# A fused windowed-attention and feed-forward kernel on one core: one pair of weight blocks less is decoded ahead of the feed-forward, its list opens with eight of its own steps, and two small additions move from GpSimd to VectorE

## The chip, the core and the metric

One core of one Trainium2 chip runs the whole kernel. The metric is the device time of one launch in microseconds, the median over the runs shown. The engines are TensorE (PE, with its weight loads as PEld), VectorE (DVE), ScalarE (ACT), GpSimd (POOL) and SyncE (SP, which only issues DMAs here).

## The reference

Attention over 4 batches, 8 heads, 768 positions, head size 64, with a window of 128 keys and 4 sink keys. Its output goes, as 3072 rows of 512, through a feed-forward of width 2048 with a piecewise activation:

```python
scores = scale * np.matmul(q, k.transpose(0, 1, 3, 2))
scores = np.where(is_sink | in_window, scores, -1000000000.0)
a = np.exp(scores - np.max(scores, axis=-1, keepdims=True))
a = a / (np.sum(a, axis=-1, keepdims=True) + 1e-09)
x = np.matmul(a, v)                      # -> rows of 512
h = x @ w_in
g = np.where(h >= 1, h, np.where(h <= -1, 0.0, (h + 1) ** 2 / 4))
out = g @ w_out
```

The two weight matrices arrive as 64-bit floating-point numbers.

## The kernel before, in words

**Units and chunks.** A unit is a batch, a head and a half of the queries (three tiles of 128). Eight units, all heads of one batch and half, make a chunk, and there are eight chunks. The attention of chunk c+1 runs beside the feed-forward of chunk c. Units 0 to 15 (chunks 0 and 1) are worked as eight pairs with plain fp32 matmuls (`pair_scores`, `early_transp`, `pair_r`, `pair_av`); from unit `NATIVE` = 16 on each unit is worked alone with operands split in a high and a low part (`load`, `scores`, `transp`, `av`).

**Weights.** The 64-bit weights are decoded on the chip, two blocks at a time, in 16 steps: step n is a pair of blocks of `w_in` for even n and of `w_out` for odd n. A step (`weights`, `decode_parts`, lines 158 to 218) is three integer operations on VectorE (shift L164, sign L170, tail L173), a cast on ScalarE (high part, L174) and a subtraction on VectorE (rest, L177). Its `fetch` also issues the DMA of the raw words of later steps. Steps 0 to `WFIRST`-1 are taken apart and woven by hand into `first_pairs`, where `queue` fixes the order on VectorE and ScalarE; a later step is one call, whose shift is held behind whatever VectorE work was written before it (L166).

**The opening.** `first_pairs` (L504) runs pairs 0 to 3 whole and the scores of pair 4. In round m it transposes pair m-1's probabilities, computes pair m's scores, and does half a decode step and the second half of the previous one.

**The lists.** From then on the order on TensorE is the order of the program. Two lists of (weight, step) are merged by `spread` (L615): the feed-forward's steps, and the attention's steps placed between them in proportion to their weights. For chunk 0 the feed-forward's list is `moe_steps` (four `split`s of weight 0, then for each of 16 blocks j four `stage1` steps of weight 0.49, and from j = 2 on three `stage2` steps of block j-2 of weight 0.65), and the remaining decode steps, of weight 1.0 each, are spread into it first (L657, lead 0.9). In the merged list of chunk 0 the first attention entries stand ahead of the first decode step; the first matmuls are the transposes of pair 4's first unit, then `stage1` of block 0. `stage1` of blocks 2p and 2p+1 needs decode step 2p.

**The other engines.** On VectorE, ScalarE and GpSimd a list scheduler picks the order at build time; on the chip each engine runs its instructions in that order and waits at the first that isn't ready. In PSUM, `stage1` has two banks (`h_ps`), which `pair_scores(4, ..)` uses too for two of its six score tiles.

**Around unit 16.** `scores(u, i)` (L266) ends, for the third tile, with the row sums: 1e-9 is added to the three sums on GpSimd (L289), VectorE takes reciprocals (L290) and scales the probabilities (L296, L298, L301), and `transp(u)` (L336) transposes them on TensorE. GpSimd also has the subtraction for the high and low parts of q (L263), of k for units 16 to 19 (L261, `KL_POOL`), and, for chunk 0, of the activation (L577, `GL_POOL`).

Of the kernel before, what the change touches and what calls it, by code (L numbers as in the profile page):

```python
# [13 lines left out]
ALU = mybir.AluOpType  # L14

B, H, S, D = 4, 8, 768, 64
# [3 lines left out]
CT = 3  # L20
NSINK = 4
KB = P + NSINK
NCT = DM // P
# [5 lines left out]
NATIVE = 16  # L29
# [3 lines left out]


CHECK = range(24, 24 + 2 * NJ)
WFIRST = 4
AHEAD = 2
SYNC = 4

# [1 line left out]
LEAD = 0.9  # L41
# [8 lines left out]
def attn_ffn(ctx, tc, qk, qkp, vx, vs, par, w_in, w_out, out):  # L50
    nc = tc.nc
# [12 lines left out]
    def queue(i, on=True):  # L64
        if on:
            e = i.ins.engine
            if e in queued:
                tc.add_manual_dep(i.ins, queued[e].name, mybir.DependencyInfo(
                    mybir.DependencyClass.NoSync, mybir.DependencyReason.DATA), reason="queue")
            queued[e] = i.ins  # L70
        return i
# [116 lines left out]
    def weights(n):  # L188
# [12 lines left out]
        def parts(on):  # L201
            j, i = n // 2 * 2, n % 2
            words = raw[n].rearrange("p j (c two) -> p j c two", two=2)
            if i:
                t = wpool.tile([P, 2, 2, DM], F32R, name="w")
                w_o[j:j + 2] = t[:, 0], t[:, 1]
            else:
                t = wi2[n // 2]
            return decode_parts(t, dec.tile([P, 2, DM], I32, name=f"bits{n % 2}"), words, pin=not on, on=on)
# [5 lines left out]

        if n < WFIRST:
            return fetch, lambda: parts(True)
# [48 lines left out]
    def scores(u, i):  # L266
        b, h, t0 = u
        qs, k_s = st["qk", u]
        if i == 0:
            st["p", u] = [att.tile([P, CT, 260], F32, name="p"), att.tile([P, 2 * CT], F32, name="stat")]  # L270
        p, stat = st["p", u]
        t = t0 + i
        lo = KB if t == 0 else 0
        c0 = i * KB if t0 else max(0, (i - 1) * KB)
        ps = ps_a.tile([P, 512], F32, name="ps_a")
        for j, q in enumerate(qs):
            nc.tensor.matmul(ps[:, lo:260], lhsT=q[:, i * P:(i + 1) * P], rhs=k_s[:, c0:c0 + 260 - lo],  # L277
                             start=(j == 0), stop=(j == len(qs) - 1))
        peak_i = peak[:, units.index(u), i:i + 1]
        m = (m0, m1, m2)[min(t, 2)]  # L280
        nc.vector.tensor_tensor_reduce(  # L281
            out=p[:, i, lo:260], in0=ps[:, lo:260], in1=m, scale=-0.125, scalar=3.0e38,
            op0=ALU.add, op1=ALU.min, accum_out=peak_i)
        nc.scalar.activation(p[:, i, lo:260], p[:, i, lo:260], AF.Exp, bias=peak_i, scale=-1.0,  # L284
                             accum_out=stat[:, i:i + 1])
        if i < CT - 1:
            return
        st.pop(("qk", u))
        nc.gpsimd.tensor_scalar(stat[:, CT:2 * CT], stat[:, 0:CT], 1.0e-9, None, op0=ALU.add)  # L289
        nc.vector.reciprocal(stat[:, CT:2 * CT], stat[:, CT:2 * CT])  # L290
        i0 = int(t0 == 0)

        for i in range(CT):
            r, own = stat[:, CT + i:CT + i + 1], p[:, i, KB:260]
            if t0 + i == 0:
                nc.vector.tensor_scalar(own, own, r, None, op0=ALU.mult)  # L296
            else:
                nc.vector.tensor_tensor_reduce(out=own, in0=own, in1=p[:, i, 0:P], scale=r, scalar=0.0,  # L298
                                               op0=ALU.add, op1=ALU.add, accum_out=stat[:, i:i + 1])
        sk = att.tile([P, CT * NSINK], F32, name="sk")[:, :(CT - i0) * NSINK]  # L300
        nc.vector.tensor_tensor(sk.rearrange("p (i s) -> p i s", s=NSINK), p[:, i0:, P:KB],  # L301
                                stat[:, CT + i0:2 * CT].unsqueeze(2).broadcast_to([P, CT - i0, NSINK]), op=ALU.mult)
        st["p", u] = (p, sk)
# [96 lines left out]
    def pair_values(m):  # L400
        v_s = vq[m % 2]
        for a in range(2):
            b, h, _ = units[2 * m + a]
            nc.sync.dma_start(v_s[:, :CT, a], vx[b, h, :, :CT])
            nc.sync.dma_start(v_s[:NSINK, CT, a], vs[b, h, :NSINK])

    def early_p(u):

        return (p0[u % 2] if u // 2 % 2 == 0 else pt0[u % 2][:, 5 * P:5 * P + CT * 260]).rearrange(
            "p (i c) -> p i c", c=260)  # L410
# [38 lines left out]
    def early_transp(u, part):  # L449

        p, pt = early_p(u), pt0[u % 2]
        on = u < H
        ps = ps_a.tile([P, 512], F32, name="ps_a")
        for n, (i, c) in enumerate((((0, KB), (1, 0), (1, KB)), ((2, 0), (2, KB)))[part]):
            nc.tensor.transpose(ps[:, n * P:(n + 1) * P], p[:, i, c:c + P], ident)
        if part:
            nc.tensor.transpose(ps[:NSINK, 2 * P:CT * P], p[:, CT - 1, P:KB], ident)
            queue(nc.scalar.copy(pt[:, CT * P:5 * P], ps[:, :2 * P]), on)
            queue(nc.scalar.copy(spn[u % 2][:NSINK], ps[:NSINK, 2 * P:CT * P]), on)
        else:  # L460
            queue(nc.scalar.copy(pt[:, :CT * P], ps[:, :CT * P]), on)

    def pair_av(m):

        T = CT * P
        v_s = vq[m % 2]
        ps = ps_a.tile([P, 512], F32, name="ps_a")

        terms = [(2, 4, 1, 2), (0, 0, 2, 0), (1, 2, 2, 1), None]
        for n, t in enumerate(terms):  # L470
            for a in range(2):
                k, s0, ns, i = t or (CT, 0, 1, CT - 1)
                rhs = pt0[a][:, s0 * P:(s0 + ns) * P] if t else spn[a]
                nc.tensor.matmul(ps[a * D:a * D + D, i * P:(i + ns) * P], lhsT=v_s[:, k, a], rhs=rhs,  # L474
                                 start=(n == 0), stop=(n == len(terms) - 1))
        x = xn[:, units[2 * m][1] // 2, :]
        return lambda: queue(nc.vector.tensor_tensor(x, ps[:, :T], x, op=ALU.mult), m < H // 2)
# [26 lines left out]
    def first_pairs():  # L504
        pair_load(0)
        pair_load(1)
        pair_values(0)
        d = None
        for m in range(H // 2 + 1):
            if m:  # L510
                pair_load(m + 1)
                pair_values(m)
                for u in (2 * m - 2, 2 * m - 1):
                    for part in range(2):
                        early_transp(u, part)
            if m == H // 2:
                pair_r(m - 1)
                d[2]()
                pair_av(m - 1)()
            pair_scores(m, 0)  # L520
            pair_scores(m, 1)
            if 0 < m < H // 2:
                d[2]()
            pair_scores(m, 2)
            if m:
                d[3]()
            if 0 < m < H // 2:
                pair_r(m - 1)
            pair_sums(m)
            if m < H // 2:  # L530
                wsteps[m][0]()
                d = wsteps[m][1]()
                d[0]()
                if m:
                    pair_av(m - 1)()
                d[1]()


    chunks = [(b, t) for t in (0, CT) for b in range(B)]
    last = chunks[-1][0] * S + chunks[-1][1] * P  # L540
    units = [(b, h, t0) for b, t0 in chunks for h in range(H)]
# [73 lines left out]
    def spread(a, b, lead=1.0):  # L615

        wa, wb = (sum(w for w, _ in s) for s in (a, b))
        steps, n, da, db = [], 0, 0.0, 0.0
        for step in b:
            while n < len(a) and da * lead * wb <= db * wa:  # L620
                steps.append(a[n])
                da += a[n][0]
                n += 1
            steps.append(step)
            db += step[0]
        return steps + a[n:]
# [14 lines left out]
    for c in range(len(chunks)):  # L641
        n1 = min(H * (c + 1), len(units)) + 2
        if c == 1:
            attn = [step for m in range(5, 9) for step in pair_steps(m)]
            attn += [step for n in range(NATIVE, n1) for step in attn_steps(n)]
        elif c > 1:
            attn = [step for n in range(n0, n1) for step in attn_steps(n)]
        n0 = n1
        for _, f in spread(attn, prev, LEAD) if c else [(0.0, first_pairs)]:
            f()  # L650
        if c == 1:
            early.close()
            chk.append(fast.enter_context(tc.tile_pool(name="chk", bufs=2)))
        b, t0 = chunks[c]
        prev = moe_steps(b * S + t0 * P, tail)
        if c == 0:
            prev = spread([(1.0, f) for f in wsteps[WFIRST:]], prev, WLEAD)  # L657

# [70 lines left out]
    with tc.If(other_v > 0):  # L729
        with tc.tile_pool(name="gen", bufs=1) as gen:  # L730

            for n in range(2 * NJ):
# [3 lines left out]
                m = gen.tile([P, DM], F32, name="m")  # L736
# [3 lines left out]
            for t0 in (0, CT):  # L740
# [3 lines left out]
                for i in range(CT):  # L744
                    m = keep[:, i]
# [53 lines left out]
```

## Time and profile before

| what | value |
|---|---|
| median of 3 runs | 713.11 us (712.43 to 714.05) |
| the profiled execution, its own time | 713.94 us |
| its span in the trace | 712.2 us |
| TensorE matmul busy | 688.1 us, 97% of the span |
| VectorE, ScalarE, GpSimd busy | 72%, 69%, 42% |
| mean granted TensorE clock | 0.994 of full |
| chain that ended last | PE 73%, DVE 11%, ACT 6% |

The rest of the profiled execution's time, 1.74 us, lies outside the span. A share of busy time is a mean over stages. The span has an opening of some 41 us without feed-forward matmuls, a first feed-forward stretch in which the weights are still being decoded (to some 130 us), and a long even stretch after it.

### The profile page before, as it was taken

The numbers are of one execution on the slowest core, as the hardware profiler recorded it, in microseconds if no ns is written. First come the engines' busy times: TensorE is split into PE (matmuls) and PEld (weight loads), VectorE is DVE, ScalarE is ACT, GpSimd is POOL, SyncE is SP. The second block draws the span as 40 slices with busy tenths as digits, with TensorE's granted clock in tenths as the row PEclk, the third lists the DMA queues.
The fourth block names the chain that finished last, engine by engine and source line by source line (L and its number), as shares of the span: only waits on it lengthen the run. The fifth ranks groups of instructions, "written<-read, shape, count | busy, mean of one in ns | idle before, by whom it ended". The sixth has DMA issues, their size and how long they took to land.

```text
span 712.2 us, 12391 instructions
## 1 busy us (share of the span) xinstructions
PE 688.1 (97%) x3937; PEld 611.2 (86%) x3937; DVE 512.9 (72%) x1405; ACT 489.4 (69%) x1265; POOL 296.2 (42%) x509
## 2 busy tenths in 40 slices
PE   6799998999999999999999999999999999999996
PEld 4577877999999999999899898999989999989995
DVE  7978998886767768788777778778776777632221
ACT  5876666686768777786777777777766866544332
POOL 2012444754544554456564455636554444400000
PEclk9999999999999999999999999999999999999999
DMA  8845533132144333254433443334422220001001
GB/s 266 297 159 188 177 126 102 46 103 58 50 138 136 104 111 120 73 165 128 118 99 108 118 126 118 118 119 123 123 56 60 88 60 17 8 1 46 0 1 49
DMA packets 44841, 73.04 MB, mean 103 GB/s; under 512 B 13024, under 2 KB 29408, under 8 KB 44768
## 3 DMA queue, kind: packets, MB, share of 16 engines
q1 hardware_dynamic: 41504, 59.59, 27.5%
q10 hardware_dynamic: 3264, 12.58, 4.9%
q8 instruction: 33, 0.54, 0.3%
q14 instruction: 40, 0.33, 0.1%
HBM read 65.87 MB, written 6.29 MB: 101 GB/s over the span
## 4 chain that ended last, share of the span: by engine, by line
PE 73%; DVE 11%; ACT 6%; DMA 3%; POOL 2%; issue 2%; SPq 0%; ACTq 0%; POOLq 0%; DVEq 0%
PE o_ps L585 30%; PE h_ps L566 30%; PE ps_a L383 4%; PE ps_a L277 4%; PE ps_a L336 2%; DVE bits L170 1%; DMA again<-w_in 1%; DVE bits L173 1%; DVE p L298 1%; ACT p L284 1%; DMA w<-w_in 1%; DVE g L575 1%; DVE gl L577 1%; POOL q_l L263 1%; PE ps_a L474 1%
## 5 line engine op out<-in xcount | busy, mean ns | idle before, releaser
L566 PE MATMUL h_ps<-x,wi 128*128 128x384 f32 x1536 | 310.5, 341 | 0.0
L566 PEld LDWEIGHTS h_ps<-x,wi 128*128 128x128 f32 x1536 | 264.3, 189 | 9.8 <-issue 1.5
L585 PE MATMUL o_ps<-w,gh 128*128 128x512 f32 x768 | 243.9, 398 | 0.0
L585 PE MATMUL o_ps<-w,gl 128*128 128x512 f32 x384 | 151.2, 394 | 0.9 <-DVE gl L577 0.9
L585 PEld LDWEIGHTS o_ps<-w,gh 128*128 128x128 f32 x768 | 134.1, 188 | 16.5 <-issue 1.7
L575 DVE SCALAR_TENSOR_TENSOR g<-g,h_ps 128x384 f32<-128x384 f32 x128 | 70.4, 550 | 63.9 <-ACT g L574 62.2
L573 ACT ACTIVATE g<-h_ps,half 128x384 f32<-128x384 f32 x128 | 73.9, 578 | 58.0 <-PE h_ps L566 56.9
L263 POOL TENSOR_TENSOR q_l<-r,q_h 128x384 fp32r<-128x384 f32 x48 | 50.7, 1056 | 132.1 <-ACT q_h L262 123.2
L576 ACT CAST gh<-g 128x384 fp32r<-128x384 f32 x128 | 65.6, 512 | 57.3 <-DVE g L575 56.8
L585 PEld LDWEIGHTS o_ps<-w,gl 128*128 128x128 f32 x384 | 72.0, 188 | 18.6 <-DVE gl L577 1.3
L577 DVE TENSOR_TENSOR gl<-g,gh 128x384 fp32r<-128x384 f32 x112 | 68.6, 612 | 25.3 <-ACT gh L576 24.3
L284 ACT ACTIVATE p<-p,peak 128x260 f32<-128x260 f32 (+1 forms) x144 | 71.4, 496 | 17.5 <-DVE peak L281 16.8
L261 DVE TENSOR_TENSOR k_s<-k_r,k_s 64x524 fp32r<-64x524 f32 (+1 forms) x44 | 46.4, 1054 | 40.0 <-ACT k_s L259 39.9
L574 ACT ACTIVATE g<-g 128x384 f32<-128x384 f32 x128 | 66.9, 523 | 2.1
L281 DVE CUSTOM_DVE_ANT_0 p<-ps_a,m 128x260 f32<-128x260 f32 (+1 forms) x144 | 56.6, 409 | 15.9 <-PE ps_a L277 15.1
L347 POOL TENSOR_SCALAR_AFFINE_SELECT pt<-pt 128x384 fp32r<-128x384 f32 (+1 forms) x96 | 51.0, 531 | 18.2 <-DVE pt L340 16.3
L298 DVE CUSTOM_DVE_ANT_0 p<-p,stat 128x128 f32<-128x128 f32 x128 | 55.4, 477 | 0.0
L345 POOL TENSOR_SCALAR_AFFINE_SELECT pt<-pt 128x384 fp32r<-128x384 f32 (+1 forms) x96 | 50.4, 525 | 7.1 <-ACT pt L339 3.0
L577 POOL TENSOR_TENSOR gl<-g,gh 128x384 fp32r<-128x384 f32 x16 | 22.6, 1415 | 69.0 <-ACT gh L576 65.5
L383 PEld LDWEIGHTS ps_a<-pt,v_s 128*128 128x128 f32 x304 | 46.6, 188 | 2.2
L383 PE MATMUL ps_a<-pt,v_s 128*128 128x256 f32 (+1 forms) x304 | 47.0, 275 | 0.0
L277 PE MATMUL ps_a<-k_s,q_h 128*128 128x260 f32 (+1 forms) x144 | 40.0, 278 | 0.9 <-DVE sk L342 0.9
(147 smaller groups left out, 977.2 us busy)
## 6 DMA issues: line engine op xcount, KB each, us to landing
r<-qk SPq DMA_DIRECT2D x48, 192.0 KB
k_r<-qk SPq DMA_DIRECT2D x32, 262.0 KB
again<-w_in SPq DMA_DIRECT2D x16, 512.0 KB
again<-w_out SPq DMA_DIRECT2D x16, 512.0 KB
w<-w_in ACTq DMA_DIRECT2D x6, 1024.0 KB
w<-w_out ACTq DMA_DIRECT2D x6, 1024.0 KB
out<-o SPq DMA_DIRECT2D x23, 256.0 KB
r<-vx SPq DMA_DIRECT2D x32, 128.0 KB
```

The costliest lines, as they stand in the source:

```text
L263: nc.gpsimd.tensor_tensor(q_l, q_r, q_h.bitcast(F32), op=ALU.subtract)
L277: nc.tensor.matmul(ps[:, lo:260], lhsT=q[:, i * P:(i + 1) * P], rhs=k_s[:, c0:c0 + 260 - lo], start=(j == 0), stop=(j == len(qs) - 1))
L284: nc.scalar.activation(p[:, i, lo:260], p[:, i, lo:260], AF.Exp, bias=peak_i, scale=-1.0, accum_out=stat[:, i:i + 1])
L298: nc.vector.tensor_tensor_reduce(out=own, in0=own, in1=p[:, i, 0:P], scale=r, scalar=0.0, op0=ALU.add, op1=ALU.add, accum_out=stat[:, i:i ...
L383: nc.tensor.matmul(z, lhsT=w, rhs=y, start=(n == 0), stop=(n == len(mms) - 1))
L566: nc.tensor.matmul(h_ps[:, :T], lhsT=w_i[j][:, w, ct * P:(ct + 1) * P], rhs=x[:, y, ct], start=(ct == 0 and n == 0), stop=(ct == NCT - 1 a ...
L573: nc.scalar.activation(g, h_ps[:, :T], AF.Relu, bias=half, scale=0.5)
L574: nc.scalar.activation(g, g, AF.Square)
L575: nc.vector.scalar_tensor_tensor(g, g, 1.0, h_ps[:, :T], op0=ALU.min, op1=ALU.max)
L576: nc.scalar.copy(gh, g)
L577: (nc.gpsimd if row0 == GL_POOL else nc.vector).tensor_tensor(gl, g, gh.bitcast(F32), op=ALU.subtract)
L585: nc.tensor.matmul(o_ps[tt], lhsT=gg[:, tt * P:(tt + 1) * P], rhs=w_o[j][:, w], start=(j == 0 and n == 0), stop=(j == NJ - 1 and n == 2))
```

## The change: what it does

`WFIRST` is 3 instead of 4. Decode step 3 leaves `first_pairs` and becomes the first entry of the spread decode steps, which are now 13, not 12; its fetch goes with it. Round 3 of `first_pairs` still finishes step 2, and round 4 has no decode work. The first nine entries of chunk 0's feed-forward list (decode step 3, four splits, the four `stage1` steps of block 0) are put ahead of all attention entries of chunk 1; only the rest is merged with these. For units 16 and 17 the addition of 1e-9 is done on VectorE.

```diff
-WFIRST = 4
+WFIRST = 3
...
-        nc.gpsimd.tensor_scalar(stat[:, CT:2 * CT], stat[:, 0:CT], 1.0e-9, None, op0=ALU.add)
+        (nc.vector if units.index(u) < NATIVE + 2 else nc.gpsimd).tensor_scalar(stat[:, CT:2 * CT], stat[:, 0:CT], 1.0e-9,
+                                                                               None, op0=ALU.add)
         nc.vector.reciprocal(stat[:, CT:2 * CT], stat[:, CT:2 * CT])
...
+            if m >= WFIRST and d:
+                rest = d[2:]
+                d = None
+            else:
+                rest = None
             if m == H // 2:
                 pair_r(m - 1)
-                d[2]()
                 pair_av(m - 1)()
             pair_scores(m, 0)
             pair_scores(m, 1)
-            if 0 < m < H // 2:
+            if rest:
+                rest[0]()
+            elif d:
                 d[2]()
             pair_scores(m, 2)
-            if m:
+            if rest:
+                rest[1]()
+            elif d:
                 d[3]()
             if 0 < m < H // 2:
                 pair_r(m - 1)
             pair_sums(m)
-            if m < H // 2:
+            if m < WFIRST:
                 wsteps[m][0]()
                 d = wsteps[m][1]()
                 d[0]()
                 if m:
                     pair_av(m - 1)()
                 d[1]()
+            elif m < H // 2:
+                pair_av(m - 1)()
...
-        for _, f in spread(attn, prev, LEAD) if c else [(0.0, first_pairs)]:
+        head = NCT + NCT + 1 if c == 1 else 0
+        for _, f in prev[:head] + spread(attn, prev[head:], LEAD) if c else [(0.0, first_pairs)]:
             f()
```

## Rows read from the trace of the kernel before

**Rows 1.** The page's busy tenths in 40 slices of 17.8 us: TensorE, VectorE, and the granted TensorE clock.

```profile
PE   6799998999999999999999999999999999999996
DVE  7978998886767768788777778778776777632221
PEclk9999999999999999999999999999999999999999
```

**Rows 2.** The waits of TensorE over the whole span: us in total, times, longest.

```profile
PE o_ps L422 <- DMA q_h<-qkp: 4.8, 1, 4.8
PE ps_a L336 <- DVE p L296: 2.0, 1, 2.0
```

**Rows 3.** Busy time of each engine in one stretch, from the first feed-forward matmul to the wait before unit 16's transposes.

```profile
41.50:119.76 78.26, 78.08 (x480) 62.47 (x479) 70.60 (x119) 52.76 (x134) 28.16 (x19) 1.00 0.43 147
```

**Rows 4.** TensorE in order of time (start, length, in brackets the idle time before and what ended it): the end of pair 4's scores, the transposes of its first unit, `stage1` of block 0.

```profile
39.44 0.38 PE L422 MATMUL ps_a<-k_s,q_h 64*128 64x260 f32 x1
40.01 0.33 PE L455 MATMUL ps_a<-ident,p 128*128 128x128 f32 x1 [0.19 <-ACT p L438]
41.30 0.44 PE L455 MATMUL ps_a<-ident,p 128*128 128x128 f32 x2 [0.96 <-ACT p L438]
41.50 0.77 PE L566 MATMUL h_ps<-x,wi 128*128 128x384 f32 x3
```

**Rows 5.** VectorE in the same stretch: the read of the first `h_ps` bank of pair 4's scores, the rest of decode step 3, the split of the last quarter of x, the shift of decode step 4.

```profile
39.90 0.42 DVE L433 CUSTOM_DVE_ANT_0 p<-h_ps,m1n 128x260 f32<-128x260 f32 x1
...
40.95 1.22 DVE L177 TENSOR_TENSOR w<-bits,w 128x1024 fp32r<-128x1024 f32 x1
42.09 0.55 DVE L597 TENSOR_TENSOR x<-xn,x 128x384 fp32r<-128x384 f32 x1
...
43.45 0.65 DVE L164 TENSOR_SCALAR bits<-w 128x1024 int32<-128x1024 int32 x1
```

**Rows 6.** The decode operations of VectorE in the stretch of rows 3, grouped: count, busy us, mean ns, idle time before.

```profile
L173 DVE SCALAR_TENSOR_TENSOR bits<-w,bits 128x1024 int32<-128x1024 int32 x11 | 16.2, 1469 | 0.2
L170 DVE SCALAR_TENSOR_TENSOR bits<-w,bits 128x1024 int32<-128x1024 int32 x11 | 15.8, 1432 | 0.2
L177 DVE TENSOR_TENSOR wi<-bits,wi 128x1024 fp32r<-128x1024 f32 x6 | 8.2, 1360 | 3.5 <-ACT wi L174 3.5
L164 DVE TENSOR_SCALAR bits<-w 128x1024 int32<-128x1024 int32 x11 | 8.1, 734 | 0.0
L177 DVE TENSOR_TENSOR w<-bits,w 128x1024 fp32r<-128x1024 f32 x6 | 7.3, 1222 | 1.3 <-ACT w L174 1.3
```

**Rows 7.** When decode steps 10, 12 and 14 are done on VectorE (start and length of their last operation), and, on TensorE, `stage1` of blocks 10, 12 and 14, which need them.

```profile
91.51 2.04 DVE L177 TENSOR_TENSOR wi<-bits,wi 128x1024 fp32r<-128x1024 f32 x1
103.65 1.22 DVE L177 TENSOR_TENSOR wi<-bits,wi 128x1024 fp32r<-128x1024 f32 x1 [0.77 <-ACT wi L174]
117.55 1.22 DVE L177 TENSOR_TENSOR wi<-bits,wi 128x1024 fp32r<-128x1024 f32 x1
...
97.02 1.21 PE L566 MATMUL h_ps<-x,wi 128*128 128x384 f32 x6
108.94 1.20 PE L566 MATMUL h_ps<-x,wi 128*128 128x384 f32 x6
123.82 3.56 PE L566 MATMUL h_ps<-x,wi 128*128 128x384 f32 x12
```

**Rows 8.** Around unit 16's transposes: TensorE, then VectorE, then GpSimd, each in order of time.

```profile
119.36 0.40 PE L585 MATMUL o_ps<-w,gl 128*128 128x512 f32 x1
121.71 0.87 PE L336 MATMUL ps_a<-ident,p 128*128 128x128 f32 x3 [1.95 <-DVE p L296]
...
119.59 0.08 DVE L281 DVE_READ_ACCUMULATOR2_ANT peak<- 128x1 f32 x1
121.09 0.18 DVE L290 RECIPROCAL stat<-stat 128x3 f32<-128x3 f32 x1 [1.42 <-POOL stat L289]
121.37 0.29 DVE L296 TENSOR_SCALAR p<-p,stat 128x128 f32<-128x128 f32 x1
...
118.38 1.26 POOL L263 TENSOR_TENSOR q_l<-r,q_h 128x384 fp32r<-128x384 f32 x1 [1.58 <-ACT q_h L262]
119.72 1.02 POOL L261 TENSOR_TENSOR k_s<-k_r,k_s 64x392 fp32r<-64x392 f32 x1
120.82 0.55 POOL L289 TENSOR_SCALAR stat<-stat 128x3 f32<-128x3 f32 x2
```

**Rows 9.** An addition of 1e-9 on VectorE, of the paired path.

```profile
104.80 0.16 DVE L445 TENSOR_SCALAR stat<-stat 128x6 f32<-128x6 f32 x1
```

**Rows 10.** TensorE's busy time and granted clock (the number after the busy time) in four stretches, and the longest wait in the first and in the one that ends just before the third.

```profile
15.00:20.00 5.00, 3.42 (x32) 1.00 0.98 330
25.00:30.00 5.00, 4.22 (x43) 1.00 1.00 385
34.00:38.00 4.00, 3.76 (x27) 0.57 0.43 121
123.00:127.00 4.00, 4.00 (x15) 0.57 0.27 59
...
17.96 0.44 PE L455 MATMUL ps_a<-ident,pt 128*128 128x128 f32 x2 [1.14 <-ACT xn L488]
33.03 0.44 PE L455 MATMUL ps_a<-ident,pt 128*128 128x128 f32 x2 [1.14 <-ACT xn L488]
```

## The prediction

> **What bounds the kernel now.** I read the busy tenths first: TensorE is at 9 in nearly every slice from the third on, so whatever moves the time must change TensorE's work or its few gaps [rows 1]. The work is the same after the change; only gaps can move. The list of its waits shows two that stand out: 4.8 us at the very start for the first load, which the change does not touch, and 2.0 us before L336 [rows 2]. The other gaps lie in the opening, where TensorE is at 6 and 7 tenths and VectorE at 7 to 9. The windows then show that between 41.50 and 119.76 us TensorE is busy for 78.08 of 78.26 us and VectorE for 70.60, 90% [rows 3]: any stage in which the feed-forward runs is bound by TensorE, with VectorE close behind while weights are decoded. Last I looked at the granted clock. It falls to half twice while there is work: around 34 to 38 us and around 123 to 127 us, each time behind a wait [rows 10].
>
> **The opening.** Step 3 leaves the hand-woven rounds, with its three integer operations, its cast, its subtraction and the DMA issues of its fetch. Most of that lay beside TensorE's chain of transposes and copies and shortens nothing. What is on the path is the join at 40 us. TensorE ends pair 4's scores at 39.82 (39.44 + 0.38), then stands idle 0.19 and 0.96 us for ScalarE's exponentials before it reaches the feed-forward at 41.50 [rows 4]. After the change the four `stage1` steps of block 0 stand ahead of those transposes. They need an `h_ps` bank, which VectorE reads out until 40.32 (39.90 + 0.42) [rows 5]. So the idle time shrinks from 1.15 to 0.50 us: a gain of 0.65. The last quarter of x must be split by the time the fourth step comes: VectorE is free for it at 40.95, since step 3's L177 is no longer there, and 41.50 (40.95 + 0.55) is early enough, because nine matmuls of 0.20 us (1.20 / 6 in [rows 7]) from 40.32 last to 42.1. Ends: 0 if the bank or the split comes late, 1.15 if nothing is waited for. The transposes that now come behind `stage1` find their exponentials done; their later users are some microseconds away.
>
> The fetch that moves issues two DMAs on ScalarE's queue for words of steps 4 and 5. Step 4 is now needed later, so I cost the move at nothing; the cover is that later position, and if it were gone step 4's shift would wait for its data. SyncE's loads for pair 6 and the values of pair 5 also come behind nine more steps; both are used much later, and I cost them at nothing too.
>
> **The added decode in the feed-forward's stretch.** One more step costs VectorE 1.47 + 1.43 + 0.73 us and, for L177, 1.29 us (15.5 us over 12): 4.93 us [rows 6]. Two additions like L445 add 0.16 us each [rows 9]. VectorE idles 7.66 us of this stretch (78.26 - 70.60) [rows 3], so there is room for 5.25 us; but 4.8 us of that idle time are waits for the cast ahead of L177 [rows 6], which come again with every step. If none of them is filled, only 2.86 us are free and VectorE ends 2.4 us behind its place.
>
> Who would notice is `stage1` of an even block. From the planner's weights: the list weighs 58.66 (64 times 0.49 and 42 times 0.65); with lead 0.9 a decode step comes every 4.40 of weight before (12 steps) and every 4.06 after (13). Step 10 stood 8.8 ahead of block 10 and now stands 6.8 ahead; step 12 goes from 7.8 to 6.5, step 14 from 6.8 to 6.2. The stretch of rows 3 holds 50.2 of weight (56 `stage1` and 35 `stage2` steps) in 78.26 us, 1.56 us for 1.0, so the three lose some 3.1, 2.0 and 1.0 us of lead. They had 3.47 us (93.55 to 97.02), 4.07 and 5.05 [rows 7]. Step 10 keeps 0.35 us, the others two or more. With VectorE 1.5 us late by step 10 (7 of 11 steps of the 2.4) TensorE would wait 1.2 us there; with the waits for casts filled, none. I take 0.6, the middle; the far end, if no idle time holds it, is the whole 4.93. Queued behind a late decode are VectorE's L575, which frees `h_ps`, and L433 for the scores; TensorE waits for both.
>
> **Unit 16.** TensorE ends its work at 119.76 and waits 1.95 us. VectorE has finished unit 17's score tiles at 119.67, but its reciprocal waits 1.42 us for GpSimd, whose two additions come behind two subtractions of 1.26 and 1.02 us [rows 8]. On VectorE the addition can follow at 119.67, 0.16 us long; from the reciprocal's start to the transposes are 0.62 us (121.09 to 121.71) [rows 8, 9]. That gives 120.45 instead of 121.71: 1.25 us gained, with some 0.7 us of wait left. One `stage2` step that stood behind these transposes also comes ahead of them now. Ends: 0, if the addition is placed late on VectorE; 1.95, if the wait goes whole.
>
> The Trainium skill (Perfetto Trace Analysis, Optimizing Scalar/DVE Operations) advises the reverse, handing work off VectorE, even to GpSimd, where VectorE is saturated. By it two additions would cost up to 0.3 us more; the row shows the addition late on GpSimd because of its queue, and I go by the row.
>
> **The clock behind it.** From 123 to 127 us the granted clock is 0.57, between the levels of 1.2 and 2.4 GHz, with TensorE busy throughout [rows 10]: 43% of 4.00 us, 1.7 us. In the opening a wait of 1.14 us was followed by such a fall in one round (33.03) and not in an earlier one (17.96; the clock is 1.00 from 15 to 20 us) [rows 10], and the gap of 0.96 at 41 us is followed by none, since rows 3 give 1.00 throughout. With 0.7 us left of 1.95 I expect no fall: gain 1.7. Ends: 0 and 1.7. The fall at 34 us has the same work ahead of it as before and stays.
>
> The Trainium skill (TensorE: Matmul & The Clock Gate, The HAM clock gate) says that the monitor watches how busy the engine was of late and runs on its own, not from the kernel's start. By that rule the same gap may or may not cost a fall, which the two waits of 1.14 us bear out; it is the first rival.
>
> **The sum.** -0.65 - 1.25 - 1.7 + 0.6 = -3.0 us. The profiled execution took 713.94 (span 712.2 and 1.74 around it): 710.9. It stands 0.83 above the median of the runs shown, 713.11, so I predict 710.1. After 130 us TensorE is dense and the gain is carried to the end.
>
> **The rivals.** (a) The clock falls all the same behind what is left of the wait. For it: no wait length in these rows separates fall from none. Against it: the shortest wait followed by a fall is 1.14 us. Only 1.7 is missing: -1.3, 711.8.
> (b) The change doesn't do what it says at unit 16: the addition stands on VectorE behind decode operations of up to 1.47 us, and the wait changes its owner only. For it: VectorE serves in order and is 90% busy. Against it: the addition's inputs are ready while VectorE ends unit 17's tiles. Then -0.65 + 0.6: 713.1.
> (c) Slower: VectorE becomes the bound. The whole 4.93 us of the added step end up in TensorE's waits for L177 ahead of `stage1` of even blocks, and the clock falls once as before: 4.93 - 0.65 - 1.25 = +3.0, 716.1. It decides from some 3.3 us of such waits on (1.9 gained, 1.4 for 0.2%). For it: VectorE goes from 90% to 97%, and step 10 has 0.35 us to spare. Against it: 7.66 us of idle time.
> (d) All covers hold: no decode is late, both waits go whole, the clock stays: -1.15 - 1.95 - 1.7 = -4.8, 708.3.
>
> **How the numbers follow.** My forecast gets 0.50, (a) 0.20, (b) 0.13, (c) 0.12, (d) 0.05. 0.2% of 713.11 is 1.43 us, about what a measurement of this kernel can tell from no change: faster is below 711.7, slower above 714.5. The forecast and (d) are faster, and of (a), which lies on the edge, a little: 0.58. The rest of (a), and (b), are the same: 0.30. (c) is slower: 0.12. The range reaches from just above (d) to somewhat above (b): 708.4 to 713.9, leaving out (c) and half of (d). The likeliest case alone spans 709 to 711.4.
>
> **What would show it.** In the changed profile: twelve `stage1` matmuls of block 0 directly behind pair 4's scores, with 0.5 us idle ahead; TensorE's wait before L336 near 0.7 us, with the addition on VectorE in the releasing chain; clock 1.00 in the microseconds behind; a wait of `stage1` for L177 of some tenths near block 10. I am wrong if waits for L177 or L575 pass 1.5 us, or if the wait before L336 is still near 2 us.

## The result and the profile after

The changed kernel takes 717.77 us (median of 6 runs), the kernel before 713.4 us in 6 runs beside it: a ratio of 1.006, with a 95% interval of 1.0047 to 1.0073. It is slower by about 4.3 us, where the prediction had 710.1. The profiled execution took 717.34 us, with a span of 715.6.

The waits of TensorE over the whole span (us in total, times, longest) answer to [rows 2]:

```profile
PE o_ps L423 <- DMA q_h<-qkp: 4.7, 1, 4.7
PE ps_a L337 <- DVE p L297: 3.2, 1, 3.2
...
PE ps_a L475 <- DMA vq<-vx: 1.0, 1, 1.0
```

The wait ahead of unit 16's transposes, 2.0 us before, has not shrunk to 0.7 but grown to 3.2 (L336 of before is L337 now). TensorE in order of time, around the opening's join [rows 4] and around unit 16 [rows 8]:

```profile
39.03 0.38 PE L423 MATMUL ps_a<-k_s,q_h 64*128 64x260 f32 x1
40.41 2.35 PE L577 MATMUL h_ps<-x,wi 128*128 128x384 f32 x12 [1.00 <-DVE peak L434]
42.60 0.49 PE L456 MATMUL ps_a<-ident,p 128*128 128x128 f32 x3
...
84.03 0.49 PE L423 MATMUL ps_a<-k_s,q_h 64*128 64x128 f32 x2 [0.78 <-DVE peak L434]
...
118.46 0.33 PE L277 MATMUL ps_a<-k_s,q_h 128*128 128x128 f32 x1 [0.69 <-DVE peak L281]
121.14 0.40 PE L596 MATMUL o_ps<-w,gl 128*128 128x512 f32 x1
124.72 0.66 PE L337 MATMUL ps_a<-ident,p 128*128 128x128 f32 x2 [3.18 <-DVE p L297]
126.08 0.30 PE L337 MATMUL ps_a<-ident,p 128*128 128x128 f32 x1 [0.70 <-DVE stat L299]
126.50 3.89 PE L577 MATMUL h_ps<-x,wi 128*128 128x384 f32 x12
```

In the opening block 0's twelve `stage1` matmuls stand directly behind pair 4's scores, as planned, and start at 40.41 us instead of 41.50. From there the lead is lost. Block 14 starts at 126.50 instead of 123.82 [rows 7], so the changed kernel has gone from 1.09 us ahead to 2.68 behind. Two thirds of that fall on unit 16: 0.69 + 3.18 + 0.70 us of waits in a place that cost 1.95 before. The 0.78 at 84 us is new as well. VectorE and ScalarE show why unit 16 is late:

```profile
107.67 0.55 DVE L586 SCALAR_TENSOR_TENSOR g<-g,h_ps 128x384 f32<-128x384 f32 x1 [1.49 <-ACT g L585]
108.15 0.69 DVE L164 TENSOR_SCALAR bits<-w 128x1024 int32<-128x1024 int32 x1
...
114.93 0.55 DVE L586 SCALAR_TENSOR_TENSOR g<-g,h_ps 128x384 f32<-128x384 f32 x1
115.39 0.69 DVE L164 TENSOR_SCALAR bits<-w 128x1024 int32<-128x1024 int32 x1
116.11 2.08 DVE L170 SCALAR_TENSOR_TENSOR bits<-w,bits 128x1024 int32<-128x1024 int32 x1
...
118.68 1.21 DVE L173 SCALAR_TENSOR_TENSOR bits<-w,bits 128x1024 int32<-128x1024 int32 x1
119.82 0.41 DVE L281 CUSTOM_DVE_ANT_0 p<-ps_a,m 128x260 f32<-128x260 f32 x1
...
121.70 1.88 DVE L177 TENSOR_TENSOR wi<-bits,wi 128x1024 fp32r<-128x1024 f32 x1 [0.40 <-ACT wi L174]
123.50 0.54 DVE L586 SCALAR_TENSOR_TENSOR g<-g,h_ps 128x384 f32<-128x384 f32 x1
123.97 0.16 DVE L289 TENSOR_SCALAR stat<-stat 128x3 f32<-128x3 f32 x1
124.16 0.18 DVE L291 RECIPROCAL stat<-stat 128x3 f32<-128x3 f32 x1
124.37 0.29 DVE L297 TENSOR_SCALAR p<-p,stat 128x128 f32<-128x128 f32 x1
```

```profile
120.63 1.04 ACT L174 CAST wi<-bits 128x1024 fp32r<-128x1024 f32 x1
121.58 0.52 ACT L585 ACTIVATE g<-g 128x384 f32<-128x384 f32 x1
122.00 0.50 ACT L284 ACTIVATE p<-p,peak 128x260 f32<-128x260 f32 x1
```

The first L164 is step 13's, held behind an L586 that waits for ScalarE; it started at 105.43 before. The four decode operations further down are step 14's. Before, its shift started at 112.14 and its first three operations stood ahead of unit 16's first score read, at 115.84. Now the shift starts at 115.39, so that unit 16's first score read comes only at 118.12, behind L170, and L173 stands ahead of the third one at 119.82. Step 14's cast holds ScalarE's last exponential back to 122.00, and its L177, which waits for that cast, holds VectorE until 123.50. The addition the change moved to VectorE runs only at 123.97, 0.16 us long. On GpSimd the two subtractions ended at 122.50 (121.48 + 1.02), as early as that exponential, so the queue behind which the addition used to stand no longer set the end.

TensorE's busy time and granted clock (the number after the busy time) around that wait answer to [rows 10]; ahead of them the stretch of [rows 3], with all engines:

```profile
40.41:121.54 81.13, 79.65 (x484) 63.72 (x484) 74.01 (x124) 53.32 (x134) 27.04 (x19) 1.00 0.42 144
```

```profile
121.00:123.00 2.00, 0.53 (x3) 1.00 0.80 258
...
127.00:128.00 1.00, 1.00 (x5) 0.50 0.56 109
129.00:130.00 1.00, 1.00 (x5) 0.50 0.63 176
```

The granted clock falls to the lower level (0.50, that is 1.2 GHz) behind the wait, as it did before. In the stretch that [rows 3] shows, TensorE now idles 1.48 us (81.13 - 79.65) where it idled 0.18. Behind block 14 TensorE loses 1.2 us more, 1.1 of it between the first `stage1` of the sixth and of the seventh chunk (470 to 555 us before, 473 to 559 now), where waits of at most 0.4 us add up to 1.1 us (0.4 before). That stretch takes between 84.8 and 86.4 us in the sixteen profiles of this case, with no pattern by edit. Behind the last matmul 0.5 us come back, so the spans differ by 3.4.

### The profile page after: what moved, and what is told of

It is laid out like the page before. It is cut to its first block, busy times and chain, and to the rows that moved or that the text cites. A ratio compares the mean times of both kernels' runs of the same rounds, so it can differ in the third digit from the quotient of the medians.

```text
span 715.6 us, 12394 instructions
## 1 busy us (share of the span) xinstructions
PE 689.1 (96%) x3937; PEld 611.8 (85%) x3937; DVE 514.0 (72%) x1407; ACT 488.7 (68%) x1265; POOL 294.3 (41%) x507
## 4 chain that ended last, share of the span: by engine, by line
PE 68%; DVE 14%; ACT 6%; DMA 6%; POOL 3%; issue 2%; SPq 0%; ACTq 0%; POOLq 0%; DVEq 0%
PE o_ps L596 29%; PE h_ps L577 28%; PE ps_a L384 4%; PE ps_a L277 3%; DVE bits L170 2%; DMA vq<-vx 2%; PE ps_a L337 2%; DMA r<-qk 2%; DVE bits L173 1%; DVE p L299 1%; ACT p L284 1%; DVE g L586 1%; DMA again<-w_in 1%; POOL q_l L263 1%; DMA w<-w_in 1%
## 5 line engine op out<-in xcount | busy, mean ns | idle before, releaser
L586 DVE SCALAR_TENSOR_TENSOR g<-g,h_ps 128x384 f32<-128x384 f32 x128 | 70.4, 550 | 65.0 <-ACT g L585 63.5
L588 DVE TENSOR_TENSOR gl<-g,gh 128x384 fp32r<-128x384 f32 x112 | 69.2, 618 | 25.3 <-ACT gh L587 24.5
```

What stands on the lines that cost most here:

```text
L586: nc.vector.scalar_tensor_tensor(g, g, 1.0, h_ps[:, :T], op0=ALU.min, op1=ALU.max)
L588: (nc.gpsimd if row0 == GL_POOL else nc.vector).tensor_tensor(gl, g, gh.bitcast(F32), op=ALU.subtract)
```

## The experiments

Four theories stand in the expectations. **L** (late): steps 13 and 14 come too late in the list, are held on VectorE behind work written before them, and fall into unit 16's softmax. **W** (work): VectorE has one step too much, wherever it stands. **A**: the additions on VectorE are at fault. **H**: the leading entries are. Ratios are to the kernel before on the same chip, with 95% intervals.

**m_early** is the changed kernel with step 13 two entries and step 14 one entry earlier in the list.

```
for n, back in ((13, 2), (14, 1)):
    k = next(k for k, s in enumerate(seq) if s[1] is wsteps[n])
    seq.insert(k - back, seq.pop(k))
```

> The changed kernel with two entries of chunk 0's list moved: decode step 13 two entries earlier and step 14 one entry earlier, so that both stand ahead of the last stage1 step of blocks 11 and 12 and not behind it; nothing else. Theory L (the shift of a step is held behind the VectorE work written before it, so both steps start late, behind those blocks' activations, and step 14 falls into unit 16's softmax): TensorE's wait before unit 16's transposes falls from 3.2 us to 1 us or less, the time from 717.8 to 712 to 714.5. Theory W (VectorE has one decode step too much, wherever it stands): the wait moves, the time stays within 1 us of 717.8. Theory A (the additions on VectorE are at fault): time stays at 717.8.

Measured: 714.9 us, 1.0029 [1.0017, 1.004]. Of the 0.6% about half is gone, so L holds for that half; the time is just above the 712 to 714.5 that L had given it. The waits of TensorE:

```profile
PE o_ps L596 <- DVE w L177: 1.3, 1, 1.3
PE ps_a L337 <- DVE p L297: 1.3, 1, 1.3
```

Unit 16's wait fell from 3.2 to 1.3 us, and the clock is 1.00 from 116 to 140 us. Step 15 is now late for `stage2` of block 14. One reason is not its place in the list but the length of its last operation:

```profile
130.31 3.25 DVE L177 TENSOR_TENSOR w<-bits,w 128x1024 fp32r<-128x1024 f32 x1
```

The same operation takes 1.21 us in f_best, below. What stands beside it is told in the last section.

**u_add** puts the additions back on GpSimd; **u_head** takes the nine leading entries away.

```
- (nc.vector if units.index(u) < NATIVE + 2 else nc.gpsimd).tensor_scalar(
+ nc.gpsimd.tensor_scalar(                              # u_add
...
- for _, f in prev[:head] + spread(attn, prev[head:], LEAD) if c else ...
+ for _, f in spread(attn, prev, LEAD) if c else ...    # u_head
```

> The changed kernel with the addition of 1e-9 of units 16 and 17 back on GpSimd. Theory L: the reciprocal still comes behind the late L177 and the activation, so 717 to 718.5, as with the change. Theory W: the same. Theory A: back to about 713.5, with the wait before unit 16's transposes at 2 us or less.

> The changed kernel without the nine leading entries: the whole list of chunk 0 is merged with the attention. Theory L: step 14 still falls among unit 16's score tiles on VectorE, so 717 to 719, and the first feed-forward matmul some 1 us later than with the change. Theory W: the same 717 to 719. Theory H (putting the nine entries first moved the attention late against the decode steps): 713 to 714.5.

Measured: u_add 717.97 us, 1.0058 [1.0041, 1.0075]; u_head 718.21 us, 1.006 [1.0044, 1.0077]. Neither edit alone moves the time, so A and H are out as sole causes. In u_add the wait before the transposes is 3.0 us, about what it is with the additions on VectorE.

**u_wf** is the other half of the change: the kernel before (four pairs decoded ahead) with the leading entries and the additions.

> The kernel before with the nine leading entries and the additions on VectorE: four pairs of weight blocks are decoded ahead, so 12 steps are left in the list. Theory L: it depends on where steps 14 and 15 stand; here step 15's first two operations come ahead of unit 16's reciprocal, so the wait before unit 16's transposes is 2 to 3 us and the time 712.5 to 715. Theory W: one step less on VectorE in the stretch, so the wait is under 1 us and the time 710 to 712.

Measured: 717.84 us, 1.0067 [1.0048, 1.0085], outside what I had expected. Without the thirteenth step it is as slow as the whole change. Its wait before the transposes is the longest of all, and VectorE shows a decode step there:

```profile
PE ps_a L337 <- DVE p L297: 4.9, 1, 4.9
```

```profile
119.54 0.85 DVE L164 TENSOR_SCALAR bits<-w 128x1024 int32<-128x1024 int32 x1 [1.21 <-DMA w<-w_out]
120.43 1.94 DVE L170 SCALAR_TENSOR_TENSOR bits<-w,bits 128x1024 int32<-128x1024 int32 x1
122.29 0.42 DVE L281 CUSTOM_DVE_ANT_0 p<-ps_a,m 128x260 f32<-128x260 f32 x1
...
123.05 1.22 DVE L173 SCALAR_TENSOR_TENSOR bits<-w,bits 128x1024 int32<-128x1024 int32 x1
124.19 0.17 DVE L291 RECIPROCAL stat<-stat 128x3 f32<-128x3 f32 x1
```

The leading entries shift the spacing of the whole list, and here step 15 lands ahead of unit 16's addition and unit 17's last score reads, with a wait of 1.21 us for its own data on top. So the place of one step, not the number of steps, can cost the whole difference.

**f_best** is u_wf with step 15 one entry later; **f_pool** is f_best with the additions on GpSimd; **p_add** is the kernel before with the additions on VectorE alone.

```
for n, by in ((15, 1),):                                # f_best, f_pool
    k = next(k for k, s in enumerate(seq) if s[1] is wsteps[n])
    seq.insert(k + by, seq.pop(k))
```

> Four pairs decoded ahead, the nine leading entries, the additions on VectorE (as in u_wf), with decode step 15 moved one entry later, behind unit 16's last score tile; nothing of step 15 then stands ahead of unit 16's reciprocal. Theory L: the wait before unit 16's transposes falls from 4.9 us to 1 us or less, so 710 to 712 (u_wf 717.8). Theory H (the leading entries cost the time): stays at 716 to 718. Against m_early, which has the same order at unit 16 and one more step in the list, the difference is what the 13th step costs: 0 by Theory L alone, 2 us or more by Theory W.

> f_best (four pairs ahead, leading entries, step 15 behind unit 16's scores; the same as before within 0.15%) with the additions of units 16 and 17 on GpSimd. If the addition on VectorE is worth what the prediction took: the wait before unit 16's transposes is 1.5 to 2 us instead of 0.5, a fall of the clock follows, and it is 0.15 to 0.4% slower than before. If GpSimd is as good a place: the same as before, wait under 1 us.

> The kernel before with the additions of units 16 and 17 on VectorE and nothing else. Theory L and the reasoning of the prediction: the wait before unit 16's transposes falls from 2.0 to 0.7 us, the time by 1.2 us, or by 2.9 if the clock's fall goes too: 710.4 to 712.1. Theory A (the additions are better off on GpSimd): 713.5 to 715.

Measured: f_best 712.18 us, 0.9996 [0.9981, 1.0011]; f_pool 711.9 us, 0.9993 [0.9979, 1.0008]; p_add 711.38 us, 0.9995 [0.998, 1.001]. One entry moved by one place gives back 0.7%. The wait before unit 16's transposes in f_best:

```profile
PE ps_a L337 <- DVE p L297: 0.5, 1, 0.5
```

It is 0.9 us in f_pool and 1.1 in p_add (1.95 before), and the clock behind it does not fall in any of the three profiles. Still no time differs from the kernel before by more than its interval: p_add misses the 1.2 to 2.9 us that I had expected of it, since its interval leaves room for a gain of 1.4 at most, and between GpSimd and VectorE as the place of the additions (f_pool, f_best) nothing can be measured.

**b_late** tests L from the other side: the kernel before, with steps 13 and 14 moved behind the last `stage1` steps of blocks 11 and 12, where the changed kernel has them.

```
for n, by in ((13, 6), (14, 2)):
    k = next(k for k, s in enumerate(seq) if s[1] is wsteps[n])
    seq.insert(k + by, seq.pop(k))
```

> The kernel before, with decode steps 13 and 14 moved later in the list: behind the last stage1 step of blocks 11 and 12, where the change puts them; 12 steps, no leading entries, additions on GpSimd. Theory L: the wait before unit 16's transposes grows from 2.0 to 3 us or more, with waits for score tiles ahead of it, and the time to 715 to 718. Theory W: no more work on VectorE, so 713 to 714.

Measured: 715.73 us, 1.0045 [1.0028, 1.0061]. Nothing else was changed, so the late place alone costs most of what the change costs. Step 14's operations stand between unit 16's score reads, as in the changed kernel:

```profile
116.67 0.69 DVE L164 TENSOR_SCALAR bits<-w 128x1024 int32<-128x1024 int32 x1
...
117.48 1.99 DVE L170 SCALAR_TENSOR_TENSOR bits<-w,bits 128x1024 int32<-128x1024 int32 x1
...
119.75 1.77 DVE L173 SCALAR_TENSOR_TENSOR bits<-w,bits 128x1024 int32<-128x1024 int32 x1
```

The wait before the transposes did not grow to 3 us, however: it is 1.9, and waits of 1.1 us in all for score tiles stand ahead of it. From pair 4's last score to the next chunk's first `stage1` this profile is 1.3 us longer than that of the kernel before (97.8 against 96.4), so it shows under half of the 3.2 us by which the times differ.

**x_14** and **m_x3** leave work out, two of the three integer operations of one step (sign and tail): x_14 those of step 14 in the changed kernel, m_x3 those of step 3 in m_early.

```
 def sign():
+    if skip:                         # x_14: skip=n == 14
+        return                       # m_x3: skip=n == 3
 ...
 def tail():
-    queue(nc.vector.scalar_tensor_tensor(w, low, 29, w, ...), on)
+    if not skip:
+        queue(nc.vector.scalar_tensor_tensor(w, low, 29, w, ...), on)
```

> The changed kernel, leaving out two of the three integer operations of decode step 14 on VectorE (sign and tail, some 3.3 us there), so that blocks 14 and 15 of w_in are not the reference's. Theory L: what is left of step 14 passes ahead of unit 16's score tiles, the wait before its transposes falls from 3.2 us to 1.5 or less, and the time from 717.8 to 713.5 to 715.5. Theory W without a place: one 13th of the surplus goes, at most 1 us faster.

> m_early (the changed kernel with steps 13 and 14 ahead of their blocks' last stage1 step; 0.3% slower than before), leaving out two of the three integer operations of decode step 3 on VectorE (sign and tail, some 2.5 us at 43 to 46 us), so that blocks 2 and 3 of w_out are not the reference's. Theory L alone: nothing changes, still 0.2 to 0.4% slower than before. Theory W for what is left (VectorE, full from 45 to 110 us, is late by the added step's work): the wait of pair 7's scores near 84 us and the wait for step 15 go, within 0.15% of before.

Measured: x_14 712.98 us, 1.0011 [0.9995, 1.0027]; m_x3 715.15 us, 1.0041 [1.0025, 1.0057]. Without these two operations of step 14 the loss is gone within the interval. That alone does not tell place from work, since it takes both away. Without step 3's, at the head of the stretch, nothing comes back, although that is two and a half microseconds of VectorE's time. By W m_x3 should have gained, and it did not; the wait at 84 us went, and in its place a wait for `h_ps` turned up at 46.62 us (L581 on L590's result, 1.1 us). So it is not simply VectorE's sum of work.

**wl3_7**, **wl4_75** and **wla_75** move all steps forward by the planner's lead instead of by hand: the changed kernel with 0.7, u_wf and p_add with 0.75.

```
- WLEAD = 0.9
+ WLEAD = 0.7      # wl3_7; 0.75 in wl4_75 and wla_75
```

> The changed kernel with WLEAD 0.7 instead of 0.9: the 13 decode steps are spread over the first part of the list, so that step 15 is decoded before unit 16's chain. Theory L: the wait before unit 16's transposes is 1 us or less and the clock keeps up there: 711 to 713.5 (0.2% faster to the same as before). Theory W: the steps come even closer together, VectorE's backlog grows, TensorE waits for VectorE between 45 and 110 us by 2 us or more: 714.5 to 717.

> Four pairs decoded ahead, the nine leading entries, the additions on VectorE (as u_wf, 0.7% slower than before), with WLEAD 0.75: all 12 steps are decoded before unit 16's chain. Theory L: wait before unit 16's transposes under 1 us, 0.1 to 0.4% faster than before. Theory W: 12 steps in less time press on VectorE earlier: the same as before or up to 0.3% slower.

> The kernel before with the additions on VectorE and WLEAD 0.75, without the leading entries: only the decode steps are earlier. Theory L: as wl4_75, less what the leading entries give in the opening (0.5 to 1 us): the same as before to 0.3% faster. Theory W: the same as before or slower.

Measured: 715.3 us, 1.0039 [1.0024, 1.0053]; 714.11 us, 1.0031 [1.0016, 1.0047]; 715.8 us, 1.0054 [1.0034, 1.0074]. All three missed what L expected and came out as W had it, wl4_75 at the edge. Unit 16's wait does shrink, to 1.5 us or less, but the steps are packed closer and TensorE idles ahead of it. TensorE from 80 to 116 us, in the kernel before, then in wl3_7, then in wl4_75:

```profile
80.00:116.00 36.00, 35.82 (x223) 1.00 0.33 110
```

```profile
80.00:116.00 36.00, 32.99 (x201) 1.00 0.38 134
```

```profile
80.00:116.00 36.00, 32.82 (x203) 1.00 0.41 140
```

Three microseconds of idle time take the place of the wait removed.

**m_e9** was to settle m_early's other half: step 9 two entries later, to take away the wait of 0.78 at 84 us.

> m_early (0.3% slower than before) with decode step 9 moved two entries later, behind pair 6's last score tiles, so that its tail no longer stands between VectorE's reads of these two tiles. Theory L (place alone, also for the rest): TensorE's wait of 0.8 us before pair 7's first scores near 84 us goes, and the time falls by 0.5 to 1 us, to 0.15 to 0.25% slower than before. Theory W (the 13th step's work comes out somewhere in any case): the wait turns up elsewhere, still 0.3% slower.

Measured: 714.99 us, 1.003 [1.0017, 1.0043]. The wait at 84 us is gone, but 0.4 and 0.5 us turned up at 102.5 and 105.5 us, and the time is m_early's, as W had it.

What m_early has lost against f_best is read from TensorE's windows, f_best first. From 42 to 116 us, and from 116 to 140:

```profile
42.00:116.00 74.00, 73.63 (x453) 1.00 0.43 146
...
116.00:140.00 24.00, 22.45 (x120) 1.00 0.29 93
```

```profile
42.00:116.00 74.00, 73.22 (x452) 1.00 0.46 154
...
116.00:140.00 24.00, 20.87 (x114) 1.00 0.30 88
```

These are 0.41 and 1.58 us more idle time, 2.0 together, where the profiled executions differ by 1.7 us (714.22 against 712.49). The 1.58 are unit 16 (1.3 and 0.5 us in m_early, 0.5 in f_best) and step 15's late L177 (1.3, where f_best waits 0.8 us for L578 on GpSimd). The profile shows step 15 late for `stage2` of block 14 in m_early; a list that avoids it was not tried.

## Why the prediction was wrong

**The opening: the place was right, the gain was not.** The prediction had the idle time at the join shrink from 1.15 to 0.50 us. It shrank to 1.00:

```profile
39.46 0.55 DVE L608 TENSOR_TENSOR x<-xn,x 128x384 fp32r<-128x384 f32 x1
39.93 0.42 DVE L434 CUSTOM_DVE_ANT_0 p<-h_ps,m1n 128x260 f32<-128x260 f32 x1
```

The first `h_ps` bank came free at 40.35 (39.93 + 0.42), close to the 40.32 that the prediction gave, but by luck. Pair 4's scores ended 0.41 us earlier than before (39.03 + 0.38 against 39.82), and VectorE read the bank no earlier, because the split of x, which the prediction had put behind that read, now stands ahead of it. So of the 1.09 us by which block 0 starts early, 0.41 come from ahead of the join, 0.53 are the three transposes that now come later, and 0.15 are idle time saved, where I had 0.65.

This can be read without the opening's own differences from run to run. From the end of pair 4's scores to the start of block 12 TensorE does the same 414 matmuls in most of the kernels. That takes 69.1 to 69.2 us in the kernel before, p_add and b_late (12 steps, no leading entries), 69.0 in u_wf, f_best and f_pool (12 steps, leading entries) and 69.6 in the changed kernel, u_add, m_early and x_14 (13 steps, leading entries; m_e9 69.8, m_x3 70.1), and also in u_head (13 steps, none). So the leading entries gained 0.1 to 0.2 us, and the thirteenth step took 0.5 to 0.6 by block 12. "The gain is carried to the end" had next to nothing to carry.

**The added decode: the term that failed.** I took 0.6 us, looked for the damage in `stage1`'s waits for L177, and named block 10 as the likeliest place. By block 12 the 0.6 is right as a number, but not as a mechanism: the wait that grew in the changed kernel is the 0.78 us at 84 us, for a score tile. `stage1` never waited for L177: steps 10, 12 and 14 were ready 4.45, 3.14 and 2.92 us ahead of their blocks. What I set aside was the step's place against everything else in VectorE's order. Spacing thirteen steps instead of twelve moves steps 13 and 14 behind the last `stage1` of blocks 11 and 12; there step 13 waits with the activation ahead of it, and step 14 starts 3.25 us later (115.39 against 112.14), in the middle of unit 16. m_early and b_late give that lateness 0.3 to 0.45%, 2.2 to 3.2 us, half to three quarters of the loss. The term "+0.6" should have read some +4 to +5: 2.2 to 3.2 us for the late place at unit 16, and some 2 us for the rest of the step (m_early and m_e9 against f_best).

**Unit 16: the sign failed.** The step reads "on VectorE the addition can follow at 119.67". It followed at 123.97. The argument took VectorE's order at unit 16 from the kernel before and applied the added decode only to even blocks' `stage1`. One change moved what the other relied on. Rival (b) had this place and this mechanism, "the addition stands on VectorE behind decode operations", with 0.13, but priced it as no change, since it let the wait change its owner and not its length. In u_add the addition is back on GpSimd and the wait is 3.0 us, so in this kernel the long wait does not hang on the engine of the addition. Where the order was left alone, in p_add, the wait came down to 1.1 us, where I had worked out 0.7. The difference is in the scaling behind the reciprocal, which took 0.29 us before and here runs beside the subtraction on GpSimd that the addition no longer waits for (118.52 to 119.53 us):

```profile
118.79 0.82 DVE L297 TENSOR_SCALAR p<-p,stat 128x128 f32<-128x128 f32 x1
```

**The clock: the premise failed, and its price is open.** In this place the clock fell where the longest wait was 1.5 us or more (wla_75, u_head, b_late, the kernel before, u_add, the changed kernel, u_wf), and not where it was 1.3 or less (the other nine), each by one profile. In the opening a fall follows a wait of 1.14 us [rows 10], so this is no rule for other places. The prediction said that with the wait below 1 us the clock would stay, and so it is; the wait grew. What the missing fall is worth is open. In p_add's profile the stretch from block 12 to the next chunk's first `stage1` takes 25.1 us against 27.3 before, 2.2 less, near the 0.85 + 1.7 of my sum, and nothing of it is given back later. But over all executions p_add is only 0.05% faster, with an interval of 0.15% either way (1.1 us). One profile of each may not stand for the rest: the mean granted clock of the kernel before lies between 0.990 and 0.998 in the 35 executions beside p_add, and the fall that its profile shows at 34 to 38 us is absent from p_add's, with the same code there. How often the fall at unit 16 happens in the kernel before was not measured.

**Moved transfers: costed at nothing, and nothing shows against it.** Pair 3's values waited 1.0 us for a DMA in this profile (L475 above). Of the sixteen profiles two others have such a wait, u_head (1.1) and wla_75 (0.75), and wla_75 has the opening of the kernel before, so the change is not shown to be its cause.

**Rival (c)** said slower, at 716.1, by VectorE as the bound with waits for L177. The sign and almost the size were right, the place was not. Its condition, VectorE without room, is half true: 74.01 of 81.13 us busy is 91%, not the 97% it had, yet in m_early, m_e9 and wl3_7 no place was found that took one more step for nothing.

**What stays open.** No kernel measurably beats the kernel before; f_best, f_pool and p_add equal it. About 0.3% of the loss, m_early against f_best, comes with the thirteenth step in every place tried, and m_x3 did not give it back. From the end of pair 4's scores to the next chunk's first `stage1` the two profiles differ by 1.9 us (96.5 against 94.6): 0.6 up to block 12, 0.8 from there to block 14, 0.5 behind it. These waits were not removed one by one. In the latter two VectorE operations on the path ran long beside GpSimd: the scaling at unit 16 0.90 instead of 0.29 us, and step 15's L177 3.25 instead of 1.21. That this, and not the step's work as such, makes up much of the other half is an untested rival; a list with less on GpSimd there was not tried. Where m_x3's freed time went is open too.

## What to carry to other kernels

When filler work is spaced evenly between the steps of a latency chain, a change to the number of fillers or to the list's start moves all of them. So work out the new position of each filler against each chain in the engine's order, not only against its own consumer: one entry moved by one place was worth 0.7% here, more than any term of the sum. An edit that moves an operation onto a nearly full in-order engine must be costed with the order after the other edits, not with the order in the trace of before. The length of an operation, too, is not fixed: look at what the other engine will run beside it in its new place. And a wait that goes in the trace is not yet time that goes in the median.

## What the hardware showed that was not expected

VectorE's addition on 128x3 elements took 0.16 us in the changed kernel at 123.97, while GpSimd was idle, and six times that where it began with most of a GpSimd subtraction still to run. VectorE, then GpSimd, in f_best; then the same two engines in m_early:

```profile
119.98 0.96 DVE L289 TENSOR_SCALAR stat<-stat 128x3 f32<-128x3 f32 x1
...
119.88 1.04 POOL L261 TENSOR_TENSOR k_s<-k_r,k_s 64x392 fp32r<-64x392 f32 x1
```

```profile
123.55 0.98 DVE L289 TENSOR_SCALAR stat<-stat 128x3 f32<-128x3 f32 x1
...
123.09 1.41 POOL L588 TENSOR_TENSOR gl<-g,gh 128x384 fp32r<-128x384 f32 x1 [1.24 <-ACT gh L587]
```

In both, the addition ends within 0.03 us of the GpSimd instruction's end (120.94 and 120.92; 124.53 and 124.50). The Trainium skill (GPSIMD Engine Reference, Key points) says that the two engines share their SBUF interfaces, and names VectorE instructions with two SBUF inputs or in a 2-port mode as the ones that contend. These rows agree on the sharing, for an addition that reads a single tensor and a constant; in which mode it runs the trace does not show. In all seven cases, over six kernels, in which the addition took 0.47 to 0.98 us, it ended 0.02 to 0.03 us behind such a GpSimd subtraction; in the others it took 0.15 to 0.17. So moving the addition off GpSimd's queue did not free it from GpSimd: in f_best it still waited out the subtraction it used to stand behind.

The decode operations show it too, and there it was dear. In the changed kernel step 14's L170 takes 2.08 us and its L177 1.88 (above), where 1.23 and 1.22 is what they took in the kernel before at 113.09 and 117.55. Both began while GpSimd was at work, from 116.10 to 117.12 and from 121.48 to 122.50, and ended 1.1 us behind it. In m_early L177 of 3.25 us began at 130.31 with GpSimd busy from 129.92 to 132.47, and also ended 1.1 us behind. VectorE's score reads, which take their input from PSUM, kept their length: 0.43 us in f_best at 119.43, with GpSimd busy from 118.78 to 119.79.

The opening's own time also varies with the same code: in the profiled executions block 0 starts at 41.50 us in the kernel before, 40.29 in p_add and 43.23 in b_late, of which none touches that stretch. wla_75, with the same code there, has 40.62. Single profiles a microsecond apart there say nothing about an edit.
